# K transposed in place in four buffers, two buffers for A's V, two PSUM banks for the last projection, an earlier SyncE branch and a plan at 430 GB/s

## The chip, the cores and the metric

The kernel runs on one core of one Trainium2 chip. The metric is the time of one execution in device microseconds (us), as the median of several executions.

A ratio is the mean time of one kernel's fast runs divided by the mean time of the fast runs of the kernel before in the same rounds on the same chip. The bracket after it is its 95% interval.

Engines: PE is TensorE (matmuls), PEld its weight loads, DVE is VectorE, ACT ScalarE, POOL GpSimd, SP SyncE. SPq and PEq are the sequencers that issue the instructions of SyncE and TensorE. A PSUM bank is one of the places that matmuls write to; copying a result out of it is called its evacuation. A line number such as L865 is a line of that kernel's source.

## The reference

Two attention blocks, A and B, whose outputs are concatenated. All tensors are bf16.

```python
# A: B=16, Sq=32, D=1024, 32 query heads, 4 KV heads, Sk=1024, Dh=128
# B: the same with 32 KV heads
q = (x @ wq).reshape(B, Sq, H, Dh).transpose(0, 2, 1, 3)
scores = einsum("bhqd,bhkd->bhqk", q, k) * Dh ** -0.5     # A repeats each KV head 8 times
o = einsum("bhqk,bhkd->bhqd", softmax(scores), v)
y = o.transpose(0, 2, 1, 3).reshape(B, Sq, H * Dh) @ wo
# result: concatenate([y_A, y_B], axis=-1)
```

The inputs are drawn with a factor of 0.1, so the scores are small and the softmax is nearly uniform. A kernel with wrong scores can therefore pass the comparison with the reference.

## The kernel before

The Python code records every operation with the buffers it reads and writes. A list scheduler then plans an order for each engine from a table of durations and one assumed DMA rate. Each engine's instructions are emitted in the planned order with the necessary semaphore waits; SyncE issues all DMAs that way, so a load whose buffer isn't free holds up the loads planned behind it. The parts that the change and the argument touch:

```python
NVB_SLOTS = 3          # buffers for B's V
NKB_SLOTS = 2          # buffers for B's K as loaded
DMA_BW = 390e3         # bytes per us that the scheduler plans with
DUR = {"scoresB": 0.222, ...}          # us of one group of 8 score matmuls
...
KB_sb  = sb("KB_sb",  [P, NKB, 2, 16 * Dh], BF)    # B's K as loaded
KBt_sb = sb("KBt_sb", [P, 2,   2, 16 * Dh], BF)    # B's K transposed
VA_sb  = sb("VA_sb",  [P, NCH, Dh], BF)            # A's V as loaded, one buffer
```

B works in "quads": four heads of one batch, 128 quads in all. The K load of a quad puts 32 keys of 128 values into each partition, 1 MB. DVE then transposes 32x32 blocks. It moves 32-bit elements, so that a pair of bf16 values travels together. A key's 128 values are 64 pairs; pair number 2i + r of a key goes to block r:

```python
def st_ktrB(q, t_):                                   # twice per quad
    pr.add("dve", lambda e: e.transpose(
        KBt_sb[:, sl, t_, :].bitcast(F32).rearrange("p (s r i) -> p s r i", r=2, i=32),
        KB_sb[:, rs, t_, :].bitcast(F32).rearrange("p (s i r) -> p s r i", r=2, i=32)), ...)
```

The input is read with every second pair, the output is written with 32 pairs side by side. The scores of a quad are 32 matmuls on 32x32 tiles of the array, each with a moving operand of 512 columns. `fp` (0 to 3) picks block r and one of the two bf16 of a pair, so the columns lie two bf16 apart:

```python
def e_s(e, fp):
    f, pd = fp // 2, fp % 2
    o0 = f * 64 + pd
    for a in range(4):
        lhsT = QB_sb[32*a:32*a+32, q.m % 2, fp, q.b*Sq:(q.b+1)*Sq]
        for g in range(2):
            cg = a ^ (2 * g)
            e.matmul(ps_s[32*cg:32*cg+32, sbf, g, :]..., lhsT,
                     kt[32*a:32*a+32, g, :, :, o0:o0+63:2],        # the moving operand: stride 2
                     start=(fp == 0), stop=(fp == 3), tile_position=(32*a, 32*cg))
```

The order in which a quad's operations are recorded decides when a K buffer may be loaded again: here after its two transposes.

```python
def quadB_all(q):
    st_ktrB(q, 0); st_ktrB(q, 1)
    if t + NKB < NIT: st_dmaK(quadsB[t + NKB])       # the next load into this K buffer
    ...                                               # loads of V
    st_scores(q); st_exp(q); st_ptr(q); ...
```

At its end the program checks that every softmax sum was in range, multiplies the verdict into a flag with one small matmul (in the PSUM bank `ps_kt`), and all engines branch on that flag: over a long general program that is only run where the check fails. SyncE waits for all its DMAs ahead of that branch:

```python
def whole(name, eng):
    fast.run_engine(name, eng, fast_sems)
    eng.wait_ge(fast_sems[flag_op.eng], flag_op.sig)
    reg = eng.alloc_register("flag_" + name)
    eng.reg_load(reg, flag[0:1, 0:1])
    if name == "sp":
        fast.await_dmas(eng, fast_sems)              # 23 waits
    with eng.If_ne(reg, flag_good):
        ...                                           # the long general program
```

Of the kernel before, what the change touches and what calls it, by code (L numbers as in the profile page):

```python
# [7 lines left out]
ALU = alu_op_type.AluOpType  # L8
# [6 lines left out]
NVB_SLOTS = 3  # L15
NVB_LATE = 2
DMA_ISSUE = 0.45
NKB_SLOTS = 2
LAZY_PER_STEP = 100
LAZY_DELAY = 0  # L20
A_STEPS_FRAC = 1.0
DMA_BW = 390e3
SP_STRICT = False
SP_AHEAD = 1.5
DMA_MARGIN = {}
# [35 lines left out]
class Prog:  # L61
# [276 lines left out]
            elif op.sig is not None:  # L338
                last.then_inc(sems[op.eng], 1)

    def await_dmas(self, eng, sems):
        for k, c in sorted(self.dma_count.items()):
            eng.wait_ge(sems[k], 16 * c)


def emit_programs(nc, stack, fast, general, flag, flag_good):


    def semaphores(pr, prefix):
        return {k: stack.enter_context(nc.semaphore(prefix + k)) for k in pr.sem_names()}  # L350

    flag_op = [op for op in fast.ops if op.name == "flag"][0]
    fast_sems, general_sems = semaphores(fast, "s_"), semaphores(general, "g_")
    meet = stack.enter_context(nc.semaphore("meet"))
    engines = ("sp", "pe", "act", "dve", "pool")

    with nc.Block() as block:

        def whole(name, eng):
            fast.run_engine(name, eng, fast_sems)  # L360
            eng.wait_ge(fast_sems[flag_op.eng], flag_op.sig)
            reg = eng.alloc_register("flag_" + name)
            eng.reg_load(reg, flag[0:1, 0:1])
            if name == "sp":
                fast.await_dmas(eng, fast_sems)
            with eng.If_ne(reg, flag_good):
                eng.drain().then_inc(meet, 1)
                eng.wait_ge(meet, len(engines))
                general.run_engine(name, eng, general_sems)
                if name == "sp":  # L370
                    general.await_dmas(eng, general_sems)

        block.sync(lambda e: whole("sp", e))
        block.tensor(lambda e: whole("pe", e))
        block.scalar(lambda e: whole("act", e))
        block.vector(lambda e: whole("dve", e))
        block.gpsimd(lambda e: whole("pool", e))
# [106 lines left out]
def build(nc, pa, pb, out):  # L484
    P = 128
# [34 lines left out]
    with contextlib.ExitStack() as stack:  # L520
# [22 lines left out]
        OTA_sb = sb("OTA_sb", [P, 2, HS, P], BF)  # L543
        OTB_sb = sb("OTB_sb", [P, 2, MS, P], BF)
        KB_sb = sb("KB_sb", [P, NKB, 2, 16 * Dh], BF)
        KBt_sb = sb("KBt_sb", [P, 2, 2, 16 * Dh], BF)
        VB_sb = sb("VB_sb", [P, NVB, 4, NCH, Dh], BF)
        KA_sb = sb("KA_sb", [P, 2, NCH, Dh], BF)
        VA_sb = sb("VA_sb", [P, NCH, Dh], BF)
        KTA_sb = sb("KTA_sb", [P, 2, Sk], BF)  # L550
        P_sb = sb("P_sb", [P, Sk], BF)
        PT_sb = sb("PT_sb", [P, NCH, P], BF)
# [145 lines left out]
        def oproj(pi, blk, G):  # L698
            gp = (blk * NG + G) % 2
            nh = HS if pi == 0 else MS  # L700
            nblk = NSB if pi == 0 else NMSB
            OT = OTA_sb if pi == 0 else OTB_sb
            wo_ = woA_sb if pi == 0 else woB_sb
            wo_res = "woA" if pi == 0 else "woB"
            lazy_flush(("wo", pi, blk))
            for oh in range(NOH):
                for h0_ in range(0, nh, 2):
                    def e_op(e, oh=oh, h0_=h0_):
                        last = None
                        for hh in range(h0_, h0_ + 2):  # L710
                            last = e.matmul(ps_pj[:, 0:OUTW], OT[:, gp, hh, :], wo_[:, hh, oh * OUTW:(oh + 1) * OUTW],  # L711
                                            start=(hh == 0), stop=(hh == nh - 1))
                        return last
                    pr.add("pe", e_op, reads=[("OT", pi, gp, h0_), ("OT", pi, gp, h0_ + 1), (wo_res, h0_), (wo_res, h0_ + 1)], writes=[BK_PJ],
                           name="oprojA" if pi == 0 else "oprojB",
                           dur=0.434 * OUTW / 512, rtag={(wo_res, h0_): blk, (wo_res, h0_ + 1): blk, ("OTv", pi, gp): (blk, G)})
                a_ap = acc[:, pi, G, oh * OUTW:(oh + 1) * OUTW]
                o_ap = ost[:, pi, oh * OUTW:(oh + 1) * OUTW]
                if nblk == 1:
                    evac(o_ap, ps_pj[:, 0:OUTW], reads=[BK_PJ], writes=[BK_PJ, ("ost", pi, oh)], name="o_fin")  # L720
                elif blk == 0:
                    pr.add("act", lambda e, a_ap=a_ap: e.copy(a_ap, ps_pj[:, 0:OUTW]), reads=[BK_PJ], writes=[BK_PJ, ("acc", pi, G, oh)], name="acc0")
                elif blk < nblk - 1:
                    pr.add("dve", lambda e, a_ap=a_ap: e.tensor_tensor(a_ap, a_ap, ps_pj[:, 0:OUTW], ALU.add),  # L724
                           reads=[BK_PJ], writes=[BK_PJ, ("acc", pi, G, oh)], name="acc+")
                else:
                    pr.add("dve", lambda e, a_ap=a_ap, o_ap=o_ap: e.tensor_tensor(o_ap, a_ap, ps_pj[:, 0:OUTW], ALU.add),
                           reads=[BK_PJ, ("acc", pi, G, oh)], writes=[BK_PJ, ("ost", pi, oh)], name="accF")
                if blk == nblk - 1:
                    c0 = cols[pi] + oh * OUTW  # L730
                    pr.add("sp", lambda e, o_ap=o_ap, c0=c0: e.dma_start(out_flat[G * P:(G + 1) * P, c0:c0 + OUTW], o_ap),
                           reads=[("ost", pi, oh)], dma_key=f"out{pi}_{oh}", name="out_dma", dur=P * OUTW * 2)
# [51 lines left out]
        def st_dmaK(q):  # L784
# [6 lines left out]
            else:  # L791
                sl = q.krslot
                ksrc = pb["k"][q.b, q.h0:q.h0 + 4].rearrange("a (p s) d -> (a p) (s d)", s=32)
                pr.add("sp", lambda e: e.dma_start(KB_sb[:, sl, :, :].rearrange("p i n -> p (i n)"), ksrc), writes=[("KB", sl)], dma_key=f"kb{sl}", name="kb_dma", dur=4 * Sk * Dh * 2, wtag={("KB", sl): q.kid})

        def st_dmaV(q):
            if q.pi == 0:
                if not q.kv_new:
                    return
                sl = q.kvslot  # L800
                pr.add("sp", lambda e: e.dma_start(VA_sb[:, :, :], pa["v"][q.b, q.s].rearrange("(p c) d -> p c d", c=NCH)),
                       writes=["VA"], dma_key="va", name="va_dma", dur=Sk * Dh * 2, wtag={"VA": q.kid})
                pr.add("pool", lambda g: g.tensor_copy(VAp_sb[:, sl, :, 0:Dh], VA_sb[:, :, :]), reads=["VA"], writes=[("VAp", sl)], name="VAp_cp",  # L803
                       rtag={"VA": q.kid}, wtag={("VAp", sl): q.kid})
            else:
                sl = q.vslot
                late = [] if sl < NVB else [("wq", sl - NVB, k_) for k_ in range(WQP)]
# [17 lines left out]
                 wtag={("KTA", sl): q.kid})  # L825

        def st_ktrB(q, t_):
            sl = q.kvslot
            rs = q.krslot
            pr.add("dve", lambda e: e.transpose(KBt_sb[:, sl, t_, :].bitcast(F32).rearrange("p (s r i) -> p s r i", r=2, i=32),  # L830
                                                   KB_sb[:, rs, t_, :].bitcast(F32).rearrange("p (s i r) -> p s r i", r=2, i=32)),
                   reads=[("KB", rs)], writes=[("KBt", sl, t_)], name="KBt_tr", rtag={("KB", rs): q.kid}, wtag={("KBt", sl, t_): q.kid})

        sbuf_rr = [0]

        def st_scores(q):
# [14 lines left out]
                           tag="A%d" % q.t, rtag=dict([(("QT", q.s % 2, a), q.s) for a in range(HS)] + [(("KTA", sl), q.kid)]),  # L851
                           wtag={("Sv", sbf): q.qid})
            else:
                sl = q.kvslot
                kt = KBt_sb[:, sl, :, :].rearrange("p i (s x) -> p (i s) x", s=16).rearrange("p (sh g cl) x -> p g sh cl x", g=2, cl=4)

                def e_s(e, fp):
                    last = None
                    f, pd = fp // 2, fp % 2
                    o0 = f * 64 + pd  # L860
                    for a in range(4):
                        lhsT = QB_sb[32 * a:32 * a + 32, q.m % 2, fp, q.b * Sq:(q.b + 1) * Sq]
                        for g in range(2):
                            cg = a ^ (2 * g)
                            last = e.matmul(ps_s[32 * cg:32 * cg + 32, sbf, g, :].rearrange("p (sh cl j) -> p sh cl j", sh=4, cl=4), lhsT,  # L865
                                            kt[32 * a:32 * a + 32, g, :, :, o0:o0 + 63:2],
                                            start=(fp == 0), stop=(fp == 3), tile_position=(32 * a, 32 * cg))
                    return last
                for fp_ in range(4):
                    pr.add("pe", lambda e, fp_=fp_: e_s(e, fp_), reads=[("QB", q.m % 2, fp_), ("KBt", sl, 0), ("KBt", sl, 1)],  # L870
                           writes=BK_S[sbf], name="scoresB", dur=0.222, tag="B%d" % q.t,
                           rtag={("QB", q.m % 2, fp_): q.m, ("KBt", sl, 0): q.kid, ("KBt", sl, 1): q.kid},
                           wtag={("Sv", sbf): q.qid})

        def st_exp(q):
# [120 lines left out]
        def quadB_all(q):  # L996
            t = q.t
            st_ktrB(q, 0)
            st_ktrB(q, 1)
            if t + NKB < NIT:  # L1000
                st_dmaK(quadsB[t + NKB])
            ahead = t - 1 + NVB + (NVB_LATE if t - 1 + NVB >= T_LATE else 0)
            while t >= 1 and nv[0] <= min(ahead, NIT - 1):
                st_dmaV(quadsB[nv[0]])
                nv[0] += 1
            st_scores(q)
            st_exp(q)
            st_ptr(q)
            st_pev(q, "act")
# [161 lines left out]
```

## Time and profile before

| | before |
|---|---|
| time, median of 3 | 859.13 us (857.79 to 860.68) |
| span of the profiled execution | 857.8 us |
| DMA queue, share of 16 engines' span | 100.9% |
| PE / DVE / ACT busy | 83% / 63% / 52% |

The first lines of the page of the kernel before: busy time of each engine in us (share of the span) and instructions; the DMA busy share in 40 equal slices (9 is 90% or more); GB/s in the same slices; the load queue with packets, MB and its share of 16 engines; and the chain of waits that ended last, as shares of the span.

```profile
PE 715.8 (83%) x11971; PEld 435.6 (51%) x12098; DVE 543.6 (63%) x1115; ACT 446.3 (52%) x981; POOL 68.0 (8%) x76
...
DMA  9999999999999999999999999999999999999994
GB/s 331 379 389 412 412 412 393 411 415 406 410 404 399 413 410 412 402 395 405 414 413 407 411 412 394 404 404 413 412 413 414 404 412 412 403 410 411 412 379 167
...
q1 hardware_dynamic: 136576, 339.78, 100.9%
...
DMA 53%; PE 22%; DVE 16%; SPq 4%; issue 3%; ACT 2%; POOL 0%; DVEq 0%
```

The loads hardly ever rest, and the chain runs through them. PE has 142 us of idle time (857.8 - 715.8). The Trainium skill ("DMA: Bandwidth & Descriptors", section "Measured (HBM→SBUF, 128 partitions, SWDGE, issued from GpSimd)") gives 425 GB/s for a 16 MB transfer of a single core, on another issuing path than here, where SyncE issues; the full slices here, at 411 to 415 GB/s, are just below that figure, so by it a full slice has little to give.

The two costliest groups that the change touches, from the page of the kernel before: line, engine, operation, output and inputs, shapes, count | busy us, mean ns of one | idle us of the engine just before, and what ended it.

```profile
L830 DVE STREAM_TRANSPOSE KBt_sb<-KB_sb 128x1024 f32<-128x1024 f32 x256 | 306.8, 1227 | 87.8 <-DMA KB_sb<-in_B_k_cache_dram 78.3
...
L865 PE MATMUL ps_s<-KBt_sb,QB_sb 32*32 32x512 bf16 x4096 | 146.5, 394 | 11.7 <-ACT P_sb L888 7.5
```

One quad's 32 score matmuls in the timeline of the kernel before (start, duration, count at the end):

```profile
511.96 1.12 PE L865 MATMUL ps_s<-KBt_sb,QB_sb 32*32 32x512 bf16 x32
```

The chain of waits of the kernel before between 600 and 660 us (start, us, what): a K load, its two transposes, the next K load.

```profile
600.46 8.89 DMA KB_sb<-in_B_k_cache_dram
...
609.38 2.38 DVE KBt_sb L830 x2
...
611.78 8.91 DMA KB_sb<-in_B_k_cache_dram
```

What SyncE waited for before it could issue (us in total, times, longest), in the list of waits of the kernel before. L794 is the load of B's K, L801 that of A's V. The rows with `VAp_sb` are waits for POOL's copy of A's V, those with `KBt_sb` waits for a K buffer's transposes; a row names only what came last, and most of these waits did not empty the queue.

```profile
SPq L794 <- DVE stat L893: 107.6, 40, 7.8
SPq L794 <- DVE KBt_sb L830: 92.7, 29, 8.9
SPq L801 <- POOL VAp_sb L803: 62.4, 32, 4.6
```

Windows of the kernel before: us, busy time of PE, PEld, DVE, ACT and POOL with instruction counts, granted TensorE clock, DMA share, GB/s. In the second and third row the queue ran thin.

```profile
180.00:200.00 20.00, 16.54 (x316) 10.60 (x317) 12.17 (x28) 12.80 (x27) 2.08 (x2) 1.00 1.04 412
...
530.00:540.00 10.00, 9.69 (x185) 6.42 (x188) 8.80 (x18) 6.20 (x15) 1.59 (x2) 0.98 0.95 366
820.00:830.00 10.00, 8.56 (x150) 5.50 (x148) 6.77 (x14) 5.10 (x13) 1.19 (x2) 1.00 0.97 346
```

### The profile page before, as it was taken

What the parts mean: (1) busy time and instruction counts of PE and PEld (TensorE: products, weight loads), DVE (VectorE), ACT (ScalarE), POOL (GpSimd) and SP (SyncE); (2) the same over time, 40 slices, a digit from 0 to 9 for tenths busy, and PEclk for the clock granted to TensorE, in tenths of its full rate; (3) what the DMA queues carried; (4) which work ended last, traced back from release to release, by engine and by line L of the source; (5) the groups of instructions that cost most, each with busy time, mean ns of one, the idle gap of its engine ahead of it and who ended that gap; (6) DMA issues with size and microseconds to landing.
All of it is one profiled execution on the core that took longest, in us unless ns stands there. A gap on an engine that the chain in (4) does not pass through costs nothing.

```text
span 857.8 us, 27329 instructions
## 1 busy us (share of the span) xinstructions
PE 715.8 (83%) x11971; PEld 435.6 (51%) x12098; DVE 543.6 (63%) x1115; ACT 446.3 (52%) x981; POOL 68.0 (8%) x76
## 2 busy tenths in 40 slices
PE   3999999798978788799888878978988887878785
PEld 2556655455545455455545545545555554545452
DVE  1655666666657477567775756766776665757574
ACT  1455766465545464456544545545555464555541
POOL 0001000100000010000000000000000000000000
PEclk9999999999999899899998999999999998999998
DMA  9999999999999999999999999999999999999994
GB/s 331 379 389 412 412 412 393 411 415 406 410 404 399 413 410 412 402 395 405 414 413 407 411 412 394 404 404 413 412 413 414 404 412 412 403 410 411 412 379 167
DMA packets 136702, 341.61 MB, mean 398 GB/s; under 512 B 10624, under 2 KB 29056, under 8 KB 120192
## 3 DMA queue, kind: packets, MB, share of 16 engines
q1 hardware_dynamic: 136576, 339.78, 100.9%
q8 instruction: 97, 1.59, 0.7%
q14 instruction: 29, 0.24, 0.1%
HBM read 337.64 MB, written 2.10 MB: 396 GB/s over the span
## 4 chain that ended last, share of the span: by engine, by line
DMA 53%; PE 22%; DVE 16%; SPq 4%; issue 3%; ACT 2%; POOL 0%; DVEq 0%
DMA KB_sb<-in_B_k_cache_dram 35%; DVE KBt_sb L830 12%; DMA VB_sb<-in_B_v_cache_dram 5%; PE ps_s L865 4%; PE ps_pj L711 4%; DMA woB_sb<-in_B_wo_dram 3%; PE ps_pj L670 3%; DMA out_dram<-ost 3%; DMA woA_sb<-in_A_wo_dram 3%; DMA KA_sb<-in_A_k_cache_dram 2%; PE ps_o L958 2%; PE ps_pj L653 2%; PE ps_pt L907 2%; PE ps_kt L923 2%; PE ps_s L848 1%
## 5 line engine op out<-in xcount | busy, mean ns | idle before, releaser
L830 DVE STREAM_TRANSPOSE KBt_sb<-KB_sb 128x1024 f32<-128x1024 f32 x256 | 306.8, 1227 | 87.8 <-DMA KB_sb<-in_B_k_cache_dram 78.3
L888 ACT ACTIVATE P_sb<-ps_s 128x512 bf16<-128x512 f32 x256 | 151.8, 598 | 80.7 <-PE ps_s L865 55.6
L880 ACT ACTIVATE PTA_sb<-ps_s 128x1024 bf16<-128x1024 f32 x128 | 131.4, 1026 | 111.5 <-PE ps_s L848 92.9
L865 PE MATMUL ps_s<-KBt_sb,QB_sb 32*32 32x512 bf16 x4096 | 146.5, 394 | 11.7 <-ACT P_sb L888 7.5
L584 ACT COPY PT_sb<-ps_pt 128x512 f32<-128x512 f32 x128 | 75.0, 586 | 101.2 <-PE ps_o L958 95.1
L803 POOL COPY VAp_sb<-VA_sb 128x1024 bf16<-128x1024 bf16 x64 | 66.7, 1041 | 762.4 <-DMA VA_sb<-in_A_v_cache_dram 734.1
L907 PE MATMUL ps_pt<-id,P_sb 128*128 128x128 f32 x512 | 101.7, 304 | 7.6 <-ACT P_sb L888 4.2
L958 PE MATMUL ps_o<-VB_sb,PT_sb 128*32 128x128 bf16 x3840 | 77.5, 223 | 26.3 <-DMA VB_sb<-in_B_v_cache_dram 16.4
L907 PEld LDWEIGHTS ps_pt<-id,P_sb 128*128 128x128 f32 x512 | 81.0, 206 | 30.3 <-ACT P_sb L888 10.0
L958 PEld LDWEIGHTS ps_o<-VB_sb,PT_sb 128*32 128x32 bf16 x3840 | 57.1, 97 | 60.5 <-issue 57.4
L848 PE MATMUL ps_s<-QT_sb,KTA_sb 128*128 128x256 bf16 x512 | 82.2, 273 | 4.9 <-DVE KTA_sb L586 1.6
L923 PE MATMUL ps_kt<-VAp_sb,PTA_sb 128*128 128x129 bf16 x1024 | 78.4, 221 | 8.3 <-POOL VAp_sb L803 2.9
L923 PEld LDWEIGHTS ps_kt<-VAp_sb,PTA_sb 128*128 128x128 bf16 x1024 | 66.5, 98 | 31.4 <-POOL VAp_sb L803 13.3
L865 PEld LDWEIGHTS ps_s<-KBt_sb,QB_sb 32*32 32x32 bf16 x4096 | 49.1, 90 | 65.7 <-ACT P_sb L888 13.6
L974 DVE TENSOR_SCALAR OB_sb<-ps_o,rinv_all 128x128 bf16<-128x128 f32 x128 | 43.8, 342 | 48.9 <-PE ps_o L958 47.8
L711 PE MATMUL ps_pj<-woB_sb,OTB_sb 128*128 128x512 bf16 x207 | 59.8, 383 | 14.7 <-DMA woB_sb<-in_B_wo_dram 3.9
L653 PE MATMUL ps_pj<-xT_sb,wq_sb 128*128 128x512 bf16 x229 | 64.6, 392 | 8.7 <-DMA wq_sb<-in_A_wq_dram 3.1
L670 PE MATMUL ps_pj<-xT_sb,wq_sb 128*128 128x512 bf16 x237 | 64.9, 391 | 8.2 <-DMA wq_sb<-in_B_wq_dram 2.8
L711 PE MATMUL ps_pj<-woA_sb,OTA_sb 128*128 128x512 bf16 x224 | 62.2, 393 | 10.6 <-DMA woA_sb<-in_A_wo_dram 6.2
L893 DVE TENSOR_TENSOR stat<-stat 64x1 f32<-64x1 f32 x256 | 42.5, 166 | 35.7 <-ACT P_sb L888 28.3
L724 DVE TENSOR_TENSOR acc<-acc,ps_pj 128x512 f32<-128x512 f32 x64 | 42.9, 670 | 29.3 <-PE ps_pj L711 28.9
L848 PEld LDWEIGHTS ps_s<-QT_sb,KTA_sb 128*128 128x128 bf16 x512 | 44.6, 98 | 27.8 <-ACT PTA_sb L880 5.2
(51 smaller groups left out, 542.5 us busy)
## 6 DMA issues: line engine op xcount, KB each, us to landing
KB_sb<-in_B_k_cache_dram SPq DMA_DIRECT2D x128, 1024.0 KB, 9.1
VB_sb<-in_B_v_cache_dram SPq DMA_DIRECT2D x240, 512.0 KB, 10.0
KA_sb<-in_A_k_cache_dram SPq DMA_DIRECT2D x64, 256.0 KB, 10.0
VA_sb<-in_A_v_cache_dram SPq DMA_DIRECT2D x64, 256.0 KB, 9.7
wq_sb<-in_B_wq_dram SPq DMA_DIRECT2D x32, 256.0 KB, 8.8
wq_sb<-in_A_wq_dram SPq DMA_DIRECT2D x32, 256.0 KB, 8.9
woB_sb<-in_B_wo_dram SPq DMA_DIRECT2D x32, 256.0 KB, 10.9
woA_sb<-in_A_wo_dram SPq DMA_DIRECT2D x32, 256.0 KB, 10.5
```

The costliest lines, as they stand in the source:

```text
L584: pr.add("act", lambda e: e.copy(dst_ap, src_ap), reads=reads, writes=writes, name=name + "@act", wtag=wtag, rtag=rtag)
L653: last = e.matmul(ps_pj[:, 0:tn], wq_sb[:, 0, j, hc * Dh:(hc + 1) * Dh], xT_sb[:, 0, j, t0:t0 + tn], start=(j == 0), stop=(j == DJ - 1))
L670: last = e.matmul(ps_pj[:, 0:NTOK], w, xT_sb[:, 1, j, :], start=(j == 0), stop=(j == DJ - 1))
L711: last = e.matmul(ps_pj[:, 0:OUTW], OT[:, gp, hh, :], wo_[:, hh, oh * OUTW:(oh + 1) * OUTW], start=(hh == 0), stop=(hh == nh - 1))
L830: pr.add("dve", lambda e: e.transpose(KBt_sb[:, sl, t_, :].bitcast(F32).rearrange("p (s r i) -> p s r i", r=2, i=32), KB_sb[:, rs, t_, :]. ...
L848: last = e.matmul(ps_s[:, sbf, c2, i * 2 * P:(i + 1) * 2 * P], KTA_sb[:, sl, c * P:(c + 1) * P], qt, start=True, stop=True)
L865: last = e.matmul(ps_s[32 * cg:32 * cg + 32, sbf, g, :].rearrange("p (sh cl j) -> p sh cl j", sh=4, cl=4), lhsT, kt[32 * a:32 * a + 32, g, ...
L880: pr.add("act", lambda e: e.activation(dst, src, ACTF.Exp, scale=scale), writes=BK_S[sbf] + [("PTA", q.half)], name="expA", rtag={("Sv", s ...
L888: pr.add("act", lambda e, src=src, dst=dst, g=g: e.activation(dst, src, ACTF.Exp, scale=scale, accum_out=st[:, g:g + 1]), writes=[BK_S[sbf ...
L907: last = e.transpose(ps_pt32[:, m * P:(m + 1) * P], p32[:, m:Sk // 2:NPK], id32[:])
L923: last = e.matmul(ps_kt[:, qh * OA0:qh * OA0 + Dh + 1], PTA_sb[:, h, c, qh * P:(qh + 1) * P], VAp_sb[:, sl, 4 * h + c, 0:Dh + 1], start=(h ...
L958: last = e.matmul(ps_o[32 * a:32 * a + 32, 0:Dh], PT_pairs[:, c // 2, 32 * (a ^ (c // 4 * 2)):32 * (a ^ (c // 4 * 2)) + 32, c % 2], v_buf( ...
```

## The change

Its intent is to keep the DMA queue fuller and the end shorter.

1. B's K is transposed in place. The memory of the two transposed buffers then serves as two more load buffers: four instead of two. A buffer comes free after the scores instead of after the transposes.
2. A's V is loaded into two buffers instead of one.
3. The second half of the last output projection goes to another PSUM bank, so that it needn't wait for the evacuation of the first half.
4. SyncE branches first and then waits, for the output stores alone.
5. The scheduler plans with 430 GB/s instead of 390.

The core of the diff (cut: the bookkeeping of buffer names, and the same `pj` at the other evacuations):

```diff
-NKB_SLOTS = 2
+NKB_SLOTS = 4
-DMA_BW = 390e3
+DMA_BW = 430e3
...
-            if name == "sp":
-                fast.await_dmas(eng, fast_sems)
             with eng.If_ne(reg, flag_good):
+                if name == "sp":
+                    fast.await_dmas(eng, fast_sems)
                 ...
+            if name == "sp":
+                fast.await_dmas(eng, fast_sems, "out")
...
-        KBt_sb = sb("KBt_sb", [P, 2, 2, 16 * Dh], BF)
-        VA_sb = sb("VA_sb", [P, NCH, Dh], BF)
+        VA_sb = sb("VA_sb", [P, 2, NCH, Dh], BF)
...
+                pj, bk = (ps_kt, BK_KT) if (oh and G == NG - 1 and blk == nblk - 1) else (ps_pj, BK_PJ)
...
-            pr.add("dve", lambda e: e.transpose(KBt_sb[...].rearrange("p (s r i) -> p s r i", r=2, i=32),
-                                                   KB_sb[...].rearrange("p (s i r) -> p s r i", r=2, i=32)), ...
+            k32 = KB_sb[:, q.krslot, t_, :].bitcast(F32).rearrange("p (s i r) -> p s r i", r=2, i=32)
+            pr.add("dve", lambda e: e.transpose(k32, k32), ...
...
-                                            kt[32 * a:32 * a + 32, g, :, :, o0:o0 + 63:2],
+                                            kt[32 * a:32 * a + 32, g, :, :, fp:Dh:4],
...
-            if t + NKB < NIT:
-                st_dmaK(quadsB[t + NKB])
             ...
             st_scores(q)
+            if t + NKB < NIT:
+                st_dmaK(quadsB[t + NKB])
```

The slice `fp:Dh:4` follows from the first item. In place, a block must be written where it was read, with every second pair; otherwise block 0 would overwrite pairs of block 1 that aren't read yet. Every second pair is every fourth bf16.

## The prediction

> **What bounds it now.** The DMA engines. The page's DMA row reads 9 in all but the last of 40 slices; packets took 100.9% of 16 engines' span. Cut into 10 us windows, 50 to 820 us shows a DMA share of 1.01 to 1.06 and 384 to 419 GB/s, except 530 to 540 (0.95, 366 GB/s). PE is busy 83%, DVE 63%, ACT 52%: they wait for data. The chain of waits alternates K load (9 us) and K transposes (2.4 us); that loop sets how deep the queue stands, and the queue is almost never empty, so more buffers cannot shorten the saturated part.
>
> **What is left to win** (estimates from the windows, against about 411 GB/s):
> - Dips where the queue ran thin: 20 to 50 us (394, 366, 366), 130, 380, 530, 820 (346). Windows 530 and 820 cost 1.1 and 1.6 us, the others 1 to 2 together. In the SyncE timeline they sit in issue gaps: 525.4 to 532.4 (waits for a K slot) and 819.4 to 824.0 (waits for the POOL copy of A's V).
> - Head, 0 to 10 us at 238 GB/s: perhaps 0.5 us.
> - Tail: loads end near 843.3, program at 857.8.
>
> **What the change does.**
> 1. K transposed in place, four buffers, same memory. K loads may stand three ahead; a slot comes free after the scores. Fills the thin spots: about -2 us.
> 2. V of A in two buffers: the SyncE waits on POOL (62 us in 32 waits, list of waits) mostly vanish; few drained the queue: about -1 us.
> 3. Two PSUM banks: the last pair of projections took 848.06 to 851.64, the second waiting for the first's evacuation. Interleaved: about -0.5 us. But the flag's matmul shares that bank, so the check follows the last evacuation: about 1.2 us moves onto the end.
> 4. SyncE's branch took 2.66 us (854.85 to its drain at 857.51), after 23 semaphore waits that began at 852.58; the output landed at 854.45. Branching first overlaps the landing; DVE's branch took 3.26 us. With the late flag, items 3 and 4 together: about -1.3 us.
> 5. Planning at 430 GB/s reorders everything. Loads arrive later than planned, so PE may meet waits in order. About 0, risk both ways.
> 6. K ahead at the end lets the last quad's scores precede its V: 0 to -3 us.
>
> Costs: the transposes now also write with an 8 byte stride (1227 ns each now), scores read every fourth bf16 instead of every second (1.06 to 1.13 us per 32). The Trainium skill ("SBUF — State Buffer", section "Door 1: The DMA port swizzle") says strides up to 8 bf16 within a 16-byte line are free; the trace has no such case yet. I expect both unchanged within 3%.
>
> **Prediction.** Span about 851.8, timed median 853 us; 80% range 847 to 858. Faster by over 2%: 0.05; within 2%: 0.93; slower: 0.02.
>
> **What would show it.** Windows 530 and 820 at about 410 GB/s; saturated windows unchanged; the POOL row gone from the SyncE waits; the chain without its K-load-to-transpose alternation; SyncE's branch before the last output lands and program end within 1.5 us after; last V load landing near 840.
>
> **What would make it wrong.** Stride 4 slowing the scores (over 1.6 us per 32) so that PE binds; the plan leaving PE waiting in order while the queue drains; a deeper queue lifting the saturated rate itself; a tail bound by compute rather than the last load.

## More of the kernel before

For the experiments, the recorded ratios come out when the first run of each kernel, the profiled one, is left out. A ratio is therefore not quite that of the two medians that are quoted.

Between rounds the median of the kernel before moved from 859.0 to 860.4 us, so kernels of different rounds are compared by their ratios.

## The result, and the profile after

| | before, same rounds | after |
|---|---|---|
| time, median of 4 | 859.9 us (857.79 to 861.28) | 865.95 us (865.08 to 866.51) |
| ratio | | 1.0072 [1.0047, 1.0096] |
| span of the profiled execution | 857.8 us | 864.3 us |

The kernel became slower by 0.7%. This is within 2%, as predicted, but in the other direction, and outside the range of 847 to 858 us. The clock is no rival: the mean granted TensorE clock was 0.970 in the profile before and 0.996 after.

The same lines of the page after:

```profile
PE 796.1 (92%) x11980; PEld 433.6 (50%) x12098; DVE 542.6 (63%) x1115; ACT 445.7 (52%) x981; POOL 67.9 (8%) x76
...
DMA  9999999999999999999999999999999999999992
GB/s 342 405 400 393 399 385 408 403 364 383 407 401 416 411 412 411 403 414 413 412 384 408 410 413 413 402 409 413 398 404 405 411 410 414 414 413 411 412 389 93
...
q1 hardware_dynamic: 136576, 339.78, 100.0%
...
PE 71%; DMA 14%; DVE 5%; ACT 3%; issue 3%; SPq 2%; POOL 0%; POOLq 0%; DVEq 0%
```

The DMA row still reads 9 nearly everywhere, and the queue's share is 100.0%. A reader who stops there concludes that nothing changed. The chain says something else: it ran through DMA for 53% of the span before, and runs through PE for 71% after. The groups, from the page after:

```profile
L833 DVE STREAM_TRANSPOSE KB_sb<-KB_sb 128x1024 f32<-128x1024 f32 x256 | 309.6, 1229 | 54.0 <-DMA KB_sb<-in_B_k_cache_dram 52.8
L865 PE MATMUL ps_s<-KB_sb,QB_sb 32*32 32x512 bf16 x4096 | 254.8, 620 | 6.1 <-DVE KB_sb L833 5.4
```

The transposes cost what they cost before (1229 ns against 1227). A score matmul shows 620 ns instead of 394. In the timeline after, a quad's 32 matmuls take twice as long:

```profile
507.47 2.03 PE L865 MATMUL ps_s<-KB_sb,QB_sb 32*32 32x512 bf16 x32
```

Over all quads the median of the block of 32 is 1.11 us before (most lie between 1.06 and 1.14) and 1.98 us after. This is 0.87 us more for each of 128 quads, an estimate of 111 us of PE time, against 142 us of idle time before. PE's total on the page rose by only 80 us. Matmul ends are modelled and some records are missing, so I don't try to close that sum; the group's own line rose by 108 us.

PE is then the engine that sets the order of events. A piece of the chain after, between 200 and 215 us, is PE work with hardly a gap ("issue" is 2.7% of it):

```profile
200.93 0.22 PE ps_s L850 x2
201.15 0.56 PE ps_o L958 x32
201.71 1.96 PE ps_s L865 x29
203.67 0.16 PE ps_o L979
```

SyncE's waits after. The POOL row has almost gone, as item 2 of the prediction said, but SyncE now waits, ahead of the loads of B's V (L814), for PE to be done with an earlier V (`ps_o L958`):

```profile
SPq L814 <- PE ps_o L958: 140.9, 53, 6.7
...
SPq L805 <- POOL VAp_sb L807: 7.7, 4, 4.1
```

The windows after. The dips at 530 and 820 us are filled, and new ones stand elsewhere, where PE is busy 97 to 99% of the time:

```profile
180.00:200.00 20.00, 19.80 (x254) 11.74 (x255) 11.77 (x25) 12.44 (x24) 3.12 (x3) 1.00 0.88 336
420.00:440.00 20.00, 19.31 (x327) 10.84 (x330) 14.04 (x30) 10.90 (x25) 2.08 (x2) 1.00 0.97 381
...
530.00:540.00 10.00, 9.47 (x160) 5.85 (x166) 8.81 (x18) 5.30 (x11) 1.04 (x1) 1.00 1.04 412
820.00:830.00 10.00, 8.43 (x129) 3.93 (x131) 6.32 (x14) 3.94 (x8) 1.04 (x1) 1.00 1.04 413
```

The difference in span splits into three, by times read from the records of the two traces:

| us | last load landed | last evacuation ended | span ended | time of that execution |
|---|---|---|---|---|
| before | 844.0 | 851.64 | 857.78 | 860.18 |
| after | 846.6 | 855.93 | 864.33 | 866.11 |

The last load lands 2.7 us later; the work from there to the last evacuation takes 1.6 us more (9.3 against 7.7); and the end of the program takes 2.3 us more (8.4 against 6.1). Together 6.6 us, the span's 6.5 within rounding.

### The profile page after: what moved, and what is told of

It is laid out like the page before. It is cut to its first block, busy times and chain, and to the rows that moved or that the text cites. A ratio compares the mean times of both kernels' runs of the same rounds, so it can differ in the third digit from the quotient of the medians.

```text
span 864.3 us, 27372 instructions
## 1 busy us (share of the span) xinstructions
PE 796.1 (92%) x11980; PEld 433.6 (50%) x12098; DVE 542.6 (63%) x1115; ACT 445.7 (52%) x981; POOL 67.9 (8%) x76
## 4 chain that ended last, share of the span: by engine, by line
PE 71%; DMA 14%; DVE 5%; ACT 3%; issue 3%; SPq 2%; POOL 0%; POOLq 0%; DVEq 0%
PE ps_s L865 23%; PE ps_pj L714 9%; PE ps_pt L907 7%; PE ps_o L958 7%; PE ps_pj L672 6%; PE ps_pj L655 6%; DMA KB_sb<-in_B_k_cache_dram 6%; PE ps_kt L923 6%; PE ps_s L850 4%; DVE KB_sb L833 3%; DMA wq_sb<-in_B_v_cache_dram 3%; DMA VA_sb<-in_A_v_cache_dram 3%; PE ps_kt L825 2%; DMA out_dram<-ost 2%; ACT P_sb L888 2%
## 5 line engine op out<-in xcount | busy, mean ns | idle before, releaser
L833 DVE STREAM_TRANSPOSE KB_sb<-KB_sb 128x1024 f32<-128x1024 f32 x256 | 309.6, 1229 | 54.0 <-DMA KB_sb<-in_B_k_cache_dram 52.8
L865 PE MATMUL ps_s<-KB_sb,QB_sb 32*32 32x512 bf16 x4096 | 254.8, 620 | 6.1 <-DVE KB_sb L833 5.4
L865 PEld LDWEIGHTS ps_s<-KB_sb,QB_sb 32*32 32x32 bf16 x4096 | 52.4, 99 | 104.4 <-issue 83.2
L958 PE MATMUL ps_o<-VB_sb,PT_sb 128*32 128x128 bf16 x3840 | 75.7, 220 | 3.7 <-issue 3.5
L958 PEld LDWEIGHTS ps_o<-VB_sb,PT_sb 128*32 128x32 bf16 x3840 | 54.9, 96 | 39.6 <-issue 28.3
L672 PE MATMUL ps_pj<-xT_sb,wq_sb 128*128 128x512 bf16 x238 | 63.3, 388 | 4.2 <-issue 1.4
L714 PE MATMUL ps_pj<-woB_sb,OTB_sb 128*128 128x512 bf16 x205 | 57.4, 380 | 7.0 <-issue 2.3
L655 PE MATMUL ps_pj<-xT_sb,wq_sb 128*128 128x512 bf16 x230 | 59.8, 379 | 2.4 <-issue 1.1
L714 PE MATMUL ps_pj<-woA_sb,OTA_sb 128*128 128x512 bf16 x222 | 58.3, 379 | 2.9 <-issue 1.0
```

Of the source, the lines that this page charges most:

```text
L655: last = e.matmul(ps_pj[:, 0:tn], wq_sb[:, 0, j, hc * Dh:(hc + 1) * Dh], xT_sb[:, 0, j, t0:t0 + tn], start=(j == 0), stop=(j == DJ - 1))
L672: last = e.matmul(ps_pj[:, 0:NTOK], w, xT_sb[:, 1, j, :], start=(j == 0), stop=(j == DJ - 1))
L714: last = e.matmul(pj[:, 0:OUTW], OT[:, gp, hh, :], wo_[:, hh, oh * OUTW:(oh + 1) * OUTW], start=(hh == 0), stop=(hh == nh - 1))
L833: pr.add("dve", lambda e: e.transpose(k32, k32), writes=[("KB", q.krslot, t_)], name="KBt_tr", rtag={("KB", q.krslot, t_): q.kid}, wtag={( ...
L865: last = e.matmul(ps_s[32 * cg:32 * cg + 32, sbf, g, :].rearrange("p (sh cl j) -> p sh cl j", sh=4, cl=4), lhsT, kt[32 * a:32 * a + 32, g, ...
L958: last = e.matmul(ps_o[32 * a:32 * a + 32, 0:Dh], PT_pairs[:, c // 2, 32 * (a ^ (c // 4 * 2)):32 * (a ^ (c // 4 * 2)) + 32, c % 2], v_buf( ...
```

## The experiments

The theory: the stride of four bf16 in the scores' moving operand nearly halves PE's rate there, and this makes PE the limit. Rivals: the plan at 430 GB/s does the harm by its order; the in-place buffer slows the reads, as one buffer is now written and read by turns; the end of the program alone is to blame.

### First batch: the stride

**1. The change with the old stride, and nothing else.** The scores read the wrong columns. All instructions stand in the same order on every engine as after; only the address step differs.

```diff
-        kt[32 * a:32 * a + 32, g, :, :, fp:Dh:4],
+        kt[32 * a:32 * a + 32, g, :, :, 64 * (fp // 2) + fp % 2:64 * (fp // 2) + fp % 2 + 63:2],
```

> The changed kernel, with the scores reading every second bf16 of the same buffer again instead of every fourth; the order of instructions on every engine is the same, and the numbers are wrong on purpose. Theory (the stride of the moving operand made the scores slow and TensorE the limit): the 32 score matmuls of a quad go back from 1.98 to about 1.1 us, TensorE busy from 92% to about 83%, the dips at 60, 110, 190, 430 and 610 us fill up, and the time falls to 853-858 us. Rival (the new order planned at 430 GB/s, or slots held until the scores, starves the queue): the time stays at 864-867 us although the scores are faster. A third view, that the in-place buffer (read by TensorE while DMA and VectorE write it) slows the scores, would leave them at 1.98 us.

Measured: 859.76 us (858.95 to 862.03), ratio 1.000 [0.9965, 1.0034], a little above the 853 to 858 us expected; the kernel before had 860.41 in these rounds. From its page:

```profile
PE 718.3 (84%) x12098; PEld 434.2 (51%) x12098; DVE 537.9 (63%) x1115; ACT 449.6 (52%) x981; POOL 68.0 (8%) x76
...
DMA 56%; PE 26%; DVE 7%; SPq 6%; issue 3%; POOL 0%; ACT 0%; POOLq 0%; DVEq 0%
...
L865 PE MATMUL ps_s<-KB_sb,QB_sb 32*32 32x512 bf16 x4096 | 142.7, 386 | 11.0 <-DVE KB_sb L833 10.4
```

The scores are back at 386 ns, PE at 84%, and the chain at DMA 56%. The stride is the cause of the loss, and the rest of the change, in this order, is worth about nothing.

**2. The kernel before with the new stride, and nothing else.** Right numbers, two separate K buffers, not in place, same order as before.

```diff
-   e.transpose(KBt_sb[...].rearrange("p (s r i) -> p s r i", r=2, i=32),
+   e.transpose(KBt_sb[...].rearrange("p (s i r) -> p s r i", r=2, i=32),
...
-        kt[32 * a:32 * a + 32, g, :, :, o0:o0 + 63:2],
+        kt[32 * a:32 * a + 32, g, :, :, fp:Dh:4],
```

> The kernel before, with only the layout of the transposed K changed, so that the scores read every fourth bf16; two buffers, plan, tail and order of instructions unchanged, numbers right. Theory: scores 1.98 us per quad, TensorE busy about 92-93%, and the time at or above that of the changed kernel, 864-880 us. Rival (order or slots): within 1 us of before, 859-860 us.

Measured: 902.65 us (900.94 to 904.28), ratio 1.0489 [1.0452, 1.0525]. From its page:

```profile
PE 77%; ACT 10%; DVE 5%; DMA 4%; issue 1%; SPq 1%; DVEq 0%
...
L865 PE MATMUL ps_s<-KBt_sb,QB_sb 32*32 32x512 bf16 x4096 | 255.0, 621 | 18.5 <-ACT P_sb L888 13.7
```

The matmul costs 621 ns without any in-place buffer, so the in-place rival falls. But the stride alone costs 42 us, and the whole change, which contains it, lost 6. Some other part of the change hides most of the stride's cost. This was not expected, and the second and third batch follow it up.

**3. The cost by stride, measured by itself.** The kernel before with the four groups of scores read at strides 1, 2, 3 and 4 (L875, L877, L879, L881), and A's query projection, on the full array, at strides 1, 2 and 4 (L656, L658, L660). Wrong numbers.

```diff
+ if fp == 0:   moving = ka[:, :, :, 0:32]        # stride 1
+ elif fp == 1: moving = ka[:, :, :, 0:63:2]      # stride 2
+ elif fp == 2: moving = ka[:, :, :, 0:94:3]      # stride 3
+ else:         moving = ka[:, :, :, 0:125:4]     # stride 4
...
+ j < 4: xflat[:, 0:512];  j < 6: xflat[:, 0:1023:2];  else: xflat[:, 0:2045:4]
```

The rule that the expectation calls the page's is the one that the prediction cites.

> A measurement, wrong numbers on purpose: in the kernel before, the four groups of eight score matmuls read K at strides of 1, 2, 3 and 4 bf16 (each on a line of its own), and A's query projection (full array, one stream of 512 columns) reads its moving operand at strides of 1, 2 and 4. If the cost comes with leaving a few elements per 16-byte line, strides 1 and 2 take 370-390 ns and strides 3 and 4 more, 4 about 620 ns, in the scores; and the full-array projection shows it as well (390 to 620). If it comes only from several streams that read one row group at once, the projection stays at about 390 ns at stride 4. If the page's rule held (free up to 8 bf16), all would be alike.

Measured (time 868.01 us, one run, state unknown, not used). Its groups, shapes kept apart:

```profile
L875 PE MATMUL ps_s<-KBt_sb,QB_sb 32*32 32x512 bf16 x1024 | 53.4, 393 | 12.7 <-ACT P_sb L902 9.8 <-DVE KBt_sb L836 2.6
L877 PE MATMUL ps_s<-KBt_sb,QB_sb 32*32 32x512 bf16 x1024 | 52.9, 388 | 0.0
L879 PE MATMUL ps_s<-KBt_sb,QB_sb 32*32 32x512 bf16 x1024 | 67.9, 503 | 0.0
L881 PE MATMUL ps_s<-KBt_sb,QB_sb 32*32 32x512 bf16 x1024 | 81.9, 611 | 0.0
...
L656 PE MATMUL ps_pj<-xT_sb,wq_sb 128*128 128x512 bf16 x128 | 36.3, 389 | 2.9 <-DMA wq_sb<-in_A_wq_dram 1.0 <-ACT QB_sb L584 0.8 <-ACT QT_sb L584 0.6
L658 PE MATMUL ps_pj<-xT_sb,wq_sb 128*128 128x512 bf16 x64 | 19.9, 391 | 1.3 <-DMA wq_sb<-in_A_wq_dram 1.3
L660 PE MATMUL ps_pj<-xT_sb,wq_sb 128*128 128x512 bf16 x64 | 34.0, 621 | 0.0
```

Strides 1 and 2 cost the same, stride 3 costs 115 ns more (503 - 388), stride 4 another 108 (611 - 503). On the full array stride 4 costs 621 ns against 389, so it isn't a matter of 32x32 tiles. These are durations of single, overlapping matmuls; from start to start, two successive ones of that projection lie 216 ns apart at stride 1 (median), 227 at stride 2 and 431 at stride 4, so that the rate at stride 4 is half of that at stride 1. The cost belongs to the stride of the moving operand. Larger strides were not measured.

**4. An attempt at a repaired version.** K stays in place, but each block takes 32 neighbouring pairs, so that the scores have stride 2 and are meant to have the right numbers. The query projection must then deliver its rows in another order; as the columns of weights that it takes are then no longer one evenly spaced set, each of its matmuls becomes four on 128x32 tiles. SyncE's wait is put back to its old place, and the check's matmul goes to a third bank (`ps_pt`).

```diff
-  k32 = KB_sb[...].rearrange("p (s i r) -> p s r i", r=2, i=32)
+  k32 = KB_sb[...].rearrange("p (s r i) -> p s r i", r=2, i=32)
...
-  w = wq_sb[:, 1, j, fp:CW:4]
-  e.matmul(ps_pj[:, 0:NTOK], w, xT_sb[:, 1, j, :], ...)
+  for a in range(4):
+      c0 = 128 * a + 64 * (fp // 2) + fp % 2
+      e.matmul(ps_pj[32*a:32*a+32, 0:NTOK], wq_sb[:, 1, j, c0:c0+63:2], xT_sb[:, 1, j, :], ..., tile_position=(0, 32*a))
...
-  e.matmul(ps_kt[0:1, 0:2], ones[:], good[:], ...)       # the check
+  e.matmul(ps_pt32[0:1, 0:2], ones[:], good[:], ...)
```

> A version meant to win, numbers right: the changed kernel with K transposed in place in contiguous 32-column blocks so that the scores read at stride 2, the query projection of B split in four 32-column tiles to match, SyncE's waits back ahead of its branch, and the check's matmul in the bank of the transposed probabilities so that it need not follow the last evacuation. Theory: scores about 1.1 us per quad, and from the last evacuation to the end about 6.1 us as in the kernel before (8.4 us in the changed one), so 2 us below the stride-2 version with the new tail: 850-856 us. If the tail change had been right as it was, this would be slower than that version.

Measured: 863.67 us (861.34 to 864.41), ratio 1.0027 [0.9993, 1.0061]. The expectation of a gain was missed. The scores took 387 ns and PE was 84% busy, so the stride was repaired; but the last load landed at 846.8 us, after thin spots that neither the kernel before nor experiment 1 has to this depth (327 GB/s in the sixth of 40 slices). Ahead of the end, the differences from experiment 1 are the extra, smaller projection matmuls, the order that the scheduler made of them and of the earlier check, and the transposes' address step (1228 ns each, as in experiment 1 with 1230); which of them made the thin spots was not separated.

### Second batch: the plan and the branch

**5. The kernel before with the plan at 430 GB/s, and nothing else.**

```diff
-DMA_BW = 390e3
+DMA_BW = 430e3
```

> The kernel before, with only the planned bandwidth raised from 390 to 430 GB/s, which changes the order of instructions on all engines. If the plan alone is worth nothing (my reading: data arrive at about 411 GB/s either way), within 2 us of before, 858-862 us. If planning above what the queue delivers starves it, 863 us or more, with dips below 370 GB/s between 50 and 820 us; if it helps, 856 us or less.

Measured: 859.67 us (858.92 to 859.95), ratio 1.0001 [0.9985, 1.0018]. With a cheap stride the plan's rate is worth nothing either way.

**6. The kernel before with SyncE branching first, and nothing else.**

```diff
-            if name == "sp":
-                fast.await_dmas(eng, fast_sems)
             with eng.If_ne(reg, flag_good):
+                if name == "sp":
+                    fast.await_dmas(eng, fast_sems)
                 ...
+            if name == "sp":
+                fast.await_dmas(eng, fast_sems, "out")
```

> The kernel before, with only SyncE's waits behind its branch. My prediction held that this saves about 2 us at the end; the trace of the changed kernel says otherwise: from the last evacuation to the end it took 8.4 us against 6.1 of before, with two fetches of instructions one after the other on SyncE. Theory now: 6.5 to 8.5 us from the last evacuation to the end here too, time the same or up to 2 us more. As predicted at first: 4 to 4.5 us, and 2 us less.

Measured: 859.17 us (858.5 to 859.63), ratio 0.9994 [0.9978, 1.0011]. The end of SyncE's program in the records of three traces (times in us from the span's start):

```
before          last store issued 851.67; 23 waits 852.58 to 854.81; branch 854.85; drain 857.51; end 857.78
branch first    branch 853.08; waits 855.77; second branch 855.92; drain 856.08; last record 858.23
after           branch 857.24; next instruction 860.66; second branch 863.95; drain 864.12; end 864.33
```

On SyncE, VectorE and ScalarE a branch's own record is short (45 to 76 ns), but the engine's next instruction starts 2.4 to 3.7 us after it, in these traces and that of experiment 1. On TensorE the record of the branch itself lasts 3.5 to 4.0 us; on GpSimd the next instruction follows after 0.16 us. Instruction packets appear on queues 8 and 14 in that time. The Trainium skill ("Runtime: NRT & Kernel Launch", section "Instruction fetch mechanics") says that a taken branch to a target outside the window of fetched pages makes the engine stop for a DMA fetch; the traces of four of the engines agree, with 2.66 us from SyncE's branch to its next instruction before and 3.42 us after. Branching first does what was intended, as the waits no longer stand ahead of the fetch. But a second stop follows in the code behind the jump: in the kernel after, 3.3 us pass between the first instruction there (860.66) and the second branch (863.95), with instruction packets again at 861.5 us; in this experiment, 2.15 us pass between the drain (856.08) and the last record (858.23). In the kernel with nothing but the branch moved, the program ended 6.1 us after the last evacuation, as before and below the 6.5 to 8.5 expected, and the timed end was 7.5 us after it instead of 8.5; the times do not show that microsecond. Each of these intervals comes from one profile.

**7. The whole change with the plan at 390 GB/s.**

```diff
-DMA_BW = 430e3
+DMA_BW = 390e3
```

> The changed kernel with the plan at 390 GB/s; its scores still read at stride 4. The kernel before with stride 4 took 902.7 us, the changed one 866: some part of the change wins back 37 us when TensorE is the limit. If it is the plan at 430 GB/s, this goes back to 885-905 us; if it is the deeper K buffers, it stays at 864-870 us.

Measured: 900.92 us (899.3 to 902.16), ratio 1.0476 [1.0459, 1.0494]; PE busy 89%, a score matmul 620 ns. Its chain of waits:

```profile
PE 78%; DVE 9%; ACT 8%; issue 3%; DMA 1%; SPq 0%; POOLq 0%; DVEq 0%
```

This answers the question from experiment 2: the plan at 430 GB/s is what hides most of the stride's cost. Without it the whole change is as slow as the stride alone.

**8. A repaired version by another way.** K is loaded 256 bytes (one key) higher in its slot and each block row is written one key lower than it was read, into places already read. The output may then have 32 pairs side by side, as in the kernel before, and the scores have stride 2. The plan is at 390 GB/s, SyncE's wait is in its old place, the check's matmul is in `ps_pt`. The two transposes of a quad must then follow one another, as the second writes over the end of the first one's input.

```diff
-  KB_sb = sb("KB_sb", [P, NKB, 2, 16 * Dh], BF)
+  KB_sb = sb("KB_sb", [P, NKB, 33 * Dh], BF)
...
-  e.dma_start(KB_sb[:, sl, :, :].rearrange("p i n -> p (i n)"), ksrc)
+  e.dma_start(KB_sb[:, sl, Dh:33 * Dh], ksrc)
...
-  k32 = KB_sb[...].rearrange("p (s i r) -> p s r i", r=2, i=32);  e.transpose(k32, k32)
+  i0 = 16 * Dh * t_
+  kin  = KB_sb[:, q.krslot, i0 + Dh:i0 + 17 * Dh].bitcast(F32).rearrange("p (s i r) -> p s r i", r=2, i=32)
+  kout = KB_sb[:, q.krslot, i0:i0 + 16 * Dh].bitcast(F32).rearrange("p (s r i) -> p s r i", r=2, i=32)
+  e.transpose(kout, kin)
```

> Meant to win, numbers right: the changed kernel with K transposed in its own slot but written 256 bytes lower than it was read, so that the result lies in contiguous 32-column blocks and the scores read at stride 2 with the query projection untouched; SyncE's waits ahead of its branch again; the check's matmul in another bank; the plan at 390 GB/s. Theory: scores about 1.1 us per quad, transposes 1.23 us, 6.1 us from the last evacuation to the end; 852-859 us. If the plan at 390 suits the four slots worse than the one at 430, 860 or more.

Measured: 858.56 us (857.26 to 859.9), ratio 0.9995 [0.9977, 1.0013]. The stride's loss is gone, and no gain is left over. The kernel is meant to be right, and it agrees with the reference; but as that comparison also lets wrong scores pass, it is no proof of the transposed K. Whoever takes this version should test it with larger inputs.

### Third batch: what to keep, and how plan and stride act together

**9 and 10. The second repaired version with SyncE branching first**, planned at 390 and at 430 GB/s.

```diff
# against experiment 8, both:
-            if name == "sp":
-                fast.await_dmas(eng, fast_sems)
             with eng.If_ne(reg, flag_good):
+                if name == "sp":
+                    fast.await_dmas(eng, fast_sems)
                 ...
+            if name == "sp":
+                fast.await_dmas(eng, fast_sems, "out")
# experiment 10 also:
-DMA_BW = 390e3
+DMA_BW = 430e3
```

> Meant to win, numbers right: the shifted in-place transpose (scores at stride 2), SyncE's branch first as in the change, but the check's matmul in another bank so that the flag is ready before the last evacuation, plan at 390 GB/s. The shifted version with the old tail had its last evacuation at 847.7 us of the profile (851.6 before), but took 9.6 us from there to the end of the timed run, against 8.5 of before and 7.5 of the kernel with only the branch moved. If these add up: about 855.5-857 us, ratio 0.996-0.998. If the fetches after the branch swallow it, 858-860.

> The same with the plan at 430 GB/s, as in the change. With TensorE no longer the limit I expect the plan to make no difference beyond 2 us: 855-859 us. If the plan at 430 is good in itself, it is the faster of the two by over 2 us.

Measured: at 390, 857.64 us (856.7 to 858.41, six runs), ratio 0.9973 [0.9957, 0.9989], the ratio as expected and the time just above; at 430, 858.3 us (857.28 to 859.2, six runs), ratio 0.9985 [0.9969, 1.0001]. The first is the fastest kernel, 0.3% faster than the kernel before, and the only one whose interval lies below 1. The reservation about the comparison holds for it too. From its page:

```profile
L835 DVE STREAM_TRANSPOSE KB_sb<-KB_sb 128x1024 f32<-128x1024 f32 x256 | 315.5, 1237 | 84.3 <-DMA KB_sb<-in_B_k_cache_dram 81.8
...
L867 PE MATMUL ps_s<-KB_sb,QB_sb 32*32 32x512 bf16 x4096 | 148.7, 397 | 11.2 <-DVE KB_sb L835 5.1
```

K can share one buffer with its transposed form at 397 ns per score matmul. So in-place buffers and the cheap stride are not opposed; only this way of writing them was.

**11. The kernel before with the new stride and the plan at 430 GB/s** (experiments 2 and 5 together).

```diff
-DMA_BW = 390e3
+DMA_BW = 430e3
# and the diff of experiment 2
```

> The kernel before with the scores at stride 4 (902.7 us) and the plan at 430 GB/s, without the deeper K buffers or the second buffer for A's V. If the plan alone wins back the 35 us: 864-872 us. If it needs the deeper buffers: 890-905 us.

Measured: 871.18 us (868.17 to 872.19), ratio 1.0125 [1.0099, 1.015]. So the plan alone wins back 31 of the 42 us of experiment 2 (of different rounds); it doesn't need the deeper buffers.

**12. The whole change at 390 GB/s, with the scores' true duration in the scheduler's table.**

```diff
-DMA_BW = 430e3
+DMA_BW = 390e3
...
-    "scoresB": 0.222, ...
+    "scoresB": 0.47, ...
```

> The changed kernel with the plan at 390 GB/s (900.9 us), but with the plan told that a group of eight score matmuls takes 0.47 us instead of 0.222. If the order at 390 was bad because the plan believed the scores cheap and let loads, not TensorE, set the pace: 860-875 us. If the plan at 390 is bad for another reason: 890 us or more.

Measured: 862.6 us (860.66 to 863.04), ratio 1.0027 [1.0005, 1.0049]. From its page:

```profile
PE 58%; DMA 30%; DVE 5%; SPq 3%; issue 2%; ACT 1%; POOLq 0%
...
L865 PE MATMUL ps_s<-KB_sb,QB_sb 32*32 32x512 bf16 x4096 | 254.8, 620 | 3.9 <-ACT P_sb L888 3.5
```

A matmul still costs 620 ns; what was won against experiment 7, 38 us (of different rounds; 1.0476 against 1.0027), came from the order alone. All runs side by side, by ratio:

| | plan at 390 GB/s | plan at 430 GB/s |
|---|---|---|
| stride 2, kernel before | 1 | 1.0001 |
| stride 4, kernel before otherwise | 1.0489 | 1.0125 |
| stride 4, the whole change | 1.0476 | 1.0072 (the change) |
| stride 4, the whole change, true score duration planned | 1.0027 | not run |
| stride 2, the whole change, shifted K, check in another bank | 0.9973 | 0.9985 |
| stride 2, the whole change, wrong columns | not run | 1.000 |

The reading: with stride 2 the plan's rate doesn't matter. With stride 4 it is worth about 4% (1.0489 against 1.0125, 1.0476 against 1.0072). The plan at 390 believes that a quad's scores take 0.89 us (four groups of 0.222) while they take 1.98, and orders PE's work as if PE had time to spare and the loads set the pace. Told the true duration, the same plan gives a far better order. A plan that believes in faster loads leans the same way, for a reason that has nothing to do with the loads. That the order alone does it is shown by experiments 7 and 12, which execute the same operations at the same cost.

Where the time goes can be read from PE's own list of waits, added up by the engine that ended each wait. PE waited for ACT and DVE together for 65.8 us in experiment 7 and 26.0 in experiment 12; for 59.0 us in experiment 2, 28.3 in experiment 11 and 28.2 in the change. These differences of 40 and 31 us are about the size of the times won back (38 and 31 us), although PE's waits for loads also grew, from 9.9 us in experiment 7 to 23.5 in experiment 12. In the slow orders PE stands still longer for results of ACT and DVE; which decisions of the scheduler make it so was not traced. The kernel before waited 59.5 us for the same two engines, but there the loads set the pace.

## Why the prediction was wrong

**The step that failed first** is the sentence on costs: "scores read every fourth bf16 instead of every second (1.06 to 1.13 us per 32) ... I expect both unchanged within 3%." The transposes were unchanged (1229 against 1227 ns). The scores went from 1.06 to 1.13 us per 32 to 1.98 us, 75% or more above instead of under 3%. The sentence rested on the Trainium skill ("SBUF — State Buffer", section "Door 1: The DMA port swizzle"), which lets strides of up to 8 bf16 go free; experiment 3 contradicts it for the moving operand of a matmul, with 388 ns at stride 2 and 611 at stride 4. The prediction also said that the trace had no such case. For a moving operand that is so, but the kernel before already loads weights at stride 4: B's query projection (L670) takes `wq_sb[:, 1, j, fp:CW:4]`, while A's (L653) takes neighbouring columns.

```profile
L670 PEld LDWEIGHTS ps_pj<-xT_sb,wq_sb 128*128 128x128 bf16 x256 | 25.2, 117 | 25.5 <-issue 4.8 <-DVE acc L724 3.5 <-DMA wq_sb<-in_B_wq_dram 3.4
...
L653 PEld LDWEIGHTS ps_pj<-xT_sb,wq_sb 128*128 128x128 bf16 x256 | 22.0, 99 | 26.8 <-issue 6.6 <-DMA wq_sb<-in_A_wq_dram 3.7 <-DVE QT_sb L586 1.2
```

A weight load took 117 ns there against 99: not free either, though much less than the moving operand's loss. The prediction named "Stride 4 slowing the scores (over 1.6 us per 32) so that PE binds" first among the things that would make it wrong. This is what happened. It gave that case no room in its 80% range, though, and with 0.9 us for 128 quads against 142 us of PE's idle time the case was both large and easy to weigh.

**"What bounds it now: the DMA engines"** was right for the kernel before, and ceased to hold with the change: from DMA 53% of the chain to PE 71%.

**Item 5, the plan, "about 0, risk both ways".** It was 0 with the old stride (ratio 1.0001), and about 35 us in favour of the change with the new one (900.92 against 865.95 us, of different rounds, or 1.0476 against 1.0072). So a fault of about 5% was seen as 0.7%. That the kernel stayed within 2%, as forecast with 0.93, was luck: planned at 390 GB/s, the same change was 4.8% slower.

**Items 1 and 2, buffers, -2 and -1 us.** The named dips at 530 and 820 us were filled in the change, and the POOL row shrank from 62.4 us in 32 waits to 7.7 in 4. But with the stride repaired and the order unchanged (experiment 1), the last load landed at 842.2 us: 1.8 us earlier than before, instead of near 840. Experiment 1's list of waits shows what SyncE waits for instead: its longest row stands ahead of the loads of B's V (L814), which got no more buffers, with 99.9 us against 37.0 in the same row before (there L810). The loads of K (L797) wait for the scores as well, with 29.5 us.

```profile
SPq L814 <- PE ps_s L865: 99.9, 44, 6.1
SPq L797 <- PE ps_s L865: 29.5, 15, 6.8
```

In experiment 1's windows a new dip stands at 180 to 200 us, and the one near 820 us came later (820 to 840 us had 373 GB/s before):

```profile
180.00:200.00 20.00, 19.13 (x321) 11.88 (x321) 12.35 (x28) 15.19 (x32) 3.13 (x3) 1.00 0.95 362
...
820.00:840.00 20.00, 16.75 (x308) 10.99 (x306) 14.20 (x32) 8.60 (x19) 2.08 (x2) 0.83 0.97 360
```

Over the windows of 20 us from 40 to 840 us the mean was 406.6 GB/s before and 406.9 in experiment 1. That the waits for V opened the new dips is likely but not shown by an experiment. The error here was to add up the dips that a change fills, without asking where the new order opens others. What four K buffers and two V buffers are worth one by one, at stride 2, was not measured; together with all the rest they make 0 to 0.3%. The buffers' worth without the in-place transposes could not be tried: a build (not a run) of the kernel before with `NKB_SLOTS` at 4, or at 3, stops because its memory for buffers is full.

**Items 3 and 4, the end, -1.3 us together.** The two banks did what was said: the last two evacuations overlap in the change (854.64 to 855.33 and 855.25 to 855.93 us), and the flag came late, as said. From the last evacuation to the timed end it took 8.54 us before, 10.18 after and 8.53 in experiment 1, which has the same instructions in the same order as the change. So the end gained nothing in the better case. What was missed is the second stop for instructions behind the jump: in the change the program ended 7.0 us after its last store landed (857.3 us), not within 1.5. The 1.65 us between the change and experiment 1 are in the two stops themselves, 3.42 and 3.29 us in the change against 2.97 and 2.09. Why such stops took from 2.1 to 3.4 us in different traces stays open. Nor does the end of the span say what an end is worth: in experiments 4 and 8, with the old wait, the program ended 6.1 and 6.0 us after the last evacuation, but the timed end came 9.3 and 9.6 us after it, later than the 8.5 of before.

**Item 6, K ahead at the end, 0 to -3 us.** From the last load to the last evacuation it took 7.7 us before, 9.3 after and 8.3 in experiment 1. It gained nothing.

**The size of the sum.** Without the stride, the predicted -6 us would still have been about 0: 859.76 against 860.41 us in the same rounds, ratio 1.000. So two things were wrong, the stride's cost, which set the sign, and the buffers' and the end's gain, which was not there.

## What to carry to other kernels

When a new layout changes the stride of an operand that the array streams, measure one group of those matmuls at the new stride before counting the memory or the buffers that it saves; here an engine that was idle for 17% of the span became the limit when one group of its matmuls took 75% longer. When an operation's cost changes, change it in the scheduler's duration table too: here the wrong entry cost 38 us, while a wrong DMA rate happened to hide it. And after a change, read the chain of waits before the busy shares, since the DMA row showed 9 throughout in both kernels while the limit had moved to another engine. Where one order of the same operations is slower than another, add up what the limiting engine waits for in each.

## What the Trainium skill lacked or had wrong

- "SBUF — State Buffer", section "Door 1: The DMA port swizzle", says that at least two hits per 16-byte line are needed for full bandwidth and gives 8 bf16 as how far one can stride for free. For the moving operand of a matmul the runs show 393 ns (stride 1), 388 (2), 503 (3) and 611 (4) on 32x32 tiles, and 389, 391 and 621 ns (1, 2, 4) on the full array. Stride 2 was free, stride 3 already was not. A weight load took 99 ns at stride 1 and 117 at stride 4. For VectorE's transposes, which came to write every second 32-bit element, the rule held (1229 against 1227 ns).
- "TensorE: Matmul & The Clock Gate", section "Step-by-step: what each phase is for", gives a matmul's throughput as one column per cycle and does not mention the stride of the streamed operand. The same 512 columns took 394 ns at stride 2 and 620 at stride 4 in these kernels; from start to start it was 216 ns at stride 1 and 431 at stride 4 on the full array (experiment 3).
- "Advanced Engine Details and Errata", section "Control Flow Timing", gives about 108 ns for a compare-and-branch. The records show 45 to 76 ns for the branch on SyncE, VectorE and ScalarE, and 2.4 to 3.7 us until the engine's next instruction where the branch jumps over a long program; on TensorE the branch's own record lasts 3.5 to 4.0 us. "Runtime: NRT & Kernel Launch", section "Instruction fetch mechanics", does describe such a stop, but without a figure, and the first section doesn't point to it.
